# Hash-masked attention and soft MoE on one core: row maxima and logit addends in PSUM, combination weights arranged with the attention, four P buffers

## The chip, the cores and the metric

The kernel runs on one core of a Trainium2 chip. The metric is device time in microseconds from one execution, the median over three runs. The engines are named as the profile names them: PE (matmuls on TensorE) with PEld (its weight loads), DVE (VectorE), ACT (ScalarE), POOL (GpSimd) and SP (SyncE, which issues nearly all transfers). Each engine takes its instructions in the order in which they are written.

## The reference

The inputs are q, k and v of 4 batches x 8 heads x 768 positions x 64 columns, a projection of 64 x 6, and the parameters of a mixture of 8 experts with 4 slots each. All of it is float32.

```python
q_bits = (einsum('bhsd,dk->bhsk', q, proj) > 0)      # k_bits likewise
mask = q_bucket[:, :, :, None] == k_bucket[:, :, None, :]
scores = where(mask, scale * q @ k.T, -1e9)
attn = exp(scores - max) / (sum + 1e-9)
x = (attn @ v)                                       # 3072 x 512, heads side by side
logits = x @ phi                                     # 3072 x 32
d = softmax of logits over the 3072 tokens
slot_input = d.T @ x                                 # 32 x 512
slot_out[e] = relu(slot_input[e] @ w1[e]) @ w2[e]    # 512 -> 1024 -> 512
c = softmax of logits over the 32 slots
out = c @ slot_out                                   # 3072 x 512
```

c are the combination weights of the change: 32 numbers for each of 3072 tokens.

## The kernel before

**Attention.** The 32 heads are worked off one after another, in pairs. A head has six row tiles of 128 positions. `smax` (L370) forms a matrix from queries, keys and hash bits, and DVE reduces each row tile of it to maxima (L373, L376); `shift` (L382 to L385) takes the maximum m of both halves and makes from it the two rows mz that are later subtracted in the matmul itself; `shift_rows` turns mz on PE (L404), casts it on ACT (L407) and moves it into the operand by DMA. `scores` (L419) then forms the scores transposed, with two matmuls each, into one of three PSUM buffers (p_st), and ACT takes the exp from there (L423) into a buffer pt of two row tiles, a P buffer. A head fills three P buffers one after the other. POOL adds the row tiles up (`acc`, L429 and L435), and PE multiplies them with v (`av`, L446). Row sums, their reciprocals and the logits' part of a pair of heads follow in `pair_sum` (L458), `pair_rec` (L465), `pair_turn` (L493), `pair_log` (L473), `pair_add` (L485, L487) and `pair_x` (L508, L510).

**Batches.** After eight heads, `batch_...` functions take that batch into the running softmax over the tokens and the running slot inputs: `batch_max`, `batch_exp` (L620, L622), `batch_turn` (L641, L643), `batch_slots` (L658, L663), and for the combination weights `batch_weigh` (L697, L698) and `batch_share` (L704 to L707). For the last batch the same chain runs behind the last head with nothing beside it: this is called the last head's gap. There 12 and 4 matmuls of `keep_warm` (L249) with unused results stand on PE.

**Soft MoE.** `hidden` (L848), a rectifier, `turned` (L862) and `model` (L930) form the slot outputs; `send` (L951) multiplies them with the combination weights and writes the output. These weights are split into a high and a low part (L878, L879), laid out with 16 bytes of each side by side (`arrange`, L887) and transposed by three matmuls per 384 columns (`turn_weights`, L893, L894), eight times, all between the matmuls of `hidden` and `model`.

**Order.** The order of work is set by hand: every step of a head has a due time in WHEN, in slots of which a head has six (`NT`), and FIRST overrides single ones. The plan is sorted by it and written out. Expert weights are loaded by `load_weights` (L229 and L231, 512 KB each) whenever SBUF becomes free near the end: wb, wy, wp, wl and wc are pools of 5, 6, 3, 5 and 1 such pieces.

**Start.** `first_y` sets constant rows in the operands by a memset (L272) and five DMAs on POOL (L274) from a row of ones; `split_lo` (L294) follows on POOL for the first pair.

Of the kernel before, what the change touches and what calls it, by code (L numbers as in the profile page):

```python
# [34 lines left out]
N_WA, N_WB, N_WY, N_WP, N_WL, N_WC = 23, 5, 6, 3, 5, 1  # L35
# [60 lines left out]
 ('one_sum', 30): 189.395,  # L96
 ('one_log', 30): 188.431,
 ('one_fold', 3): 189.992,
 ('one_turn', 30): 189.777,
 ('one_rec', 30): 190.438,  # L100
 ('one_add', 30): 190.708,
 ('one_x', 30): 191.23,
 ('one_put', 30): 192.78,
 ('acc', 31, 2): 192.109,
 ('av', 31, 2, 0): 191.864,
 ('av', 31, 2, 1): 192.733,
# [6 lines left out]
 ('bits_copy',): -13.916}  # L113
# [34 lines left out]
def lsh_attention_soft_moe(  # L148
# [56 lines left out]
    pts = [held.tile([P, 2 * S], F32, name=f"pt{j}") for j, held in enumerate((ap, lp, mp))]  # L205
# [801 lines left out]
```

## Time and profile before

| | before |
|---|---|
| median of three runs | 516.6 us (516.0 to 517.17) |
| the profiled execution's span | 515.0 us |
| its mean granted TensorE clock | 0.984 |
| PE busy | 494.8 us, 96% |
| POOL busy | 327.6 us, 64% |
| DVE busy | 381.7 us, 74% |
| ACT busy | 241.2 us, 47% |

The profiled execution's own time is its span, from the first instruction to the last; what lies around it is not in the profile. A row of a group gives the busy time and the mean of one in ns, then the engine's idle time ahead of it and what ended it. A row of a timeline gives start and length in microseconds, the instructions run together, and in brackets the idle time ahead.

### The profile page before, as it was taken

The page shows a single profiled execution, that of the slowest core. Times are in us where ns is not written, and L with a number is a line of the kernel's source. Part 1 is how long each engine was busy: PE and PEld are TensorE (multiplying, and loading weights), DVE is VectorE, ACT ScalarE, POOL GpSimd, SP SyncE. Part 2 cuts the span into 40 slices and gives each one's busy share as a digit, 9 for nine tenths or more (in the row PEclk, how much of TensorE's full clock was granted, in tenths as well). Part 3 has the DMA queues.
Part 4 walks back from the last instruction along what each step waited for, and adds up shares of the span by engine and source line. Part 5 has one row for each costly group of instructions (what it writes and reads, how often), then busy time and mean ns, then how long its engine had stood idle before and what let it go on. Part 6 is the DMA issues. An engine that isn't in the chain of part 4 may idle for free.

```text
span 515.0 us, 9100 instructions
## 1 busy us (share of the span) xinstructions
PE 494.8 (96%) x3164; PEld 289.1 (56%) x3164; DVE 381.7 (74%) x703; ACT 241.2 (47%) x463; POOL 327.6 (64%) x223
## 2 busy tenths in 40 slices
PE   6989999999999999999999999999999999999992
PEld 4555556565655555555656555555555655563562
DVE  5585877888888889797887887888877875464233
ACT  4145545454554455554564545454645545422242
POOL 9238776768676867677687867776678686512200
PEclk9789999999999999999999999999999999999997
DMA  5766766758675768586765675867455465869967
GB/s 127 203 137 151 201 161 194 175 163 192 198 161 160 185 186 196 177 191 180 180 191 140 171 197 143 229 146 222 101 145 132 93 169 197 327 264 389 409 270 277
DMA packets 39778, 99.60 MB, mean 193 GB/s; under 512 B 7458, under 2 KB 13732, under 8 KB 39732
## 3 DMA queue, kind: packets, MB, share of 16 engines
q1 hardware_dynamic: 39540, 98.94, 67.8%
q8 instruction: 25, 0.41, 0.3%
q14 instruction: 21, 0.17, 0.1%
q0 software_dynamic: 192, 0.08, 0.1%
HBM read 52.76 MB, written 6.29 MB: 115 GB/s over the span
## 4 chain that ended last, share of the span: by engine, by line
PE 78%; DVE 10%; DMA 5%; SPq 2%; ACT 2%; issue 1%; DVEq 0%; ACTq 0%
PE st L419 23%; PE av L446 21%; PE smx L370 14%; DVE mx L376 3%; PE qs L930 3%; PE qh L848 3%; DMA XY<-w 3%; DVE mx L373 2%; PE mi L458 2%; PE mi L473 2%; PE mi L328 2%; PE mi L508 2%; PE mi L404 1%; SPq L298 1%; DMA w<-w 1%
## 5 line engine op out<-in xcount | busy, mean ns | idle before, releaser
L435 POOL TENSOR_TENSOR acc<-acc,pt 128x768 f32<-128x768 f32 x125 | 238.5, 1908 | 68.5 <-ACT pt L423 54.7
L423 ACT ACTIVATE pt<-st 128x512 f32<-128x512 f32 x288 | 156.6, 596 | 60.5 <-PE st L419 49.3
L419 PE MATMUL st<-XY 128*128 128x256 f32 (+1 forms) x768 | 175.0, 342 | 0.8 <-ACT pt L423 0.5
L376 DVE TENSOR_REDUCE mx<-smx 128x1 f32<-128x512 f32 x192 | 129.4, 682 | 43.6 <-PE smx L370 43.1
L446 PE MATMUL av<-pt,v 128*64 128x384 f32 x768 | 143.1, 501 | 0.0
L419 PEld LDWEIGHTS st<-XY 128*128 128x128 f32 x768 | 123.2, 189 | 19.4 <-ACT pt L423 4.1
L370 PE MATMUL smx<-XY 96*128 96x512 f32 (+1 forms) x384 | 122.9, 374 | 5.2 <-DVE mx L376 3.9
L370 PEld LDWEIGHTS smx<-XY 96*128 96x128 f32 x384 | 65.3, 190 | 55.5 <-issue 16.4
L446 PEld LDWEIGHTS av<-pt,v 128*64 128x64 f32 x768 | 48.2, 137 | 65.7 <-issue 57.6
L429 POOL TENSOR_TENSOR acc<-pt 128x768 f32<-128x768 f32 x32 | 58.3, 1823 | 35.4 <-ACT pt L423 34.9
L373 DVE TENSOR_REDUCE mx<-smx 128x2 f32<-128x512 f32 x96 | 65.2, 679 | 8.5 <-PE smx L370 7.7
L450 ACT COPY avs<-av 128x384 f32<-128x384 f32 x32 | 15.3, 478 | 60.3 <-PE av L446 60.3
L465 DVE RECIPROCAL sm<-sm 128x128 f32<-128x128 f32 x45 | 38.4, 908 | 0.0
L294 DVE TENSOR_TENSOR w<-raw,w 128x768 fp32r<-128x768 f32 x30 | 36.3, 1210 | 1.9 <-ACT w L290 1.7
L407 ACT CAST mr<-mi 12x128 fp32r<-12x128 f32 x31 | 7.9, 254 | 62.7 <-PE mi L404 56.3
L290 ACT CAST w<-raw 128x768 fp32r<-128x768 f32 x32 | 25.1, 831 | 13.7 <-DMA v<-vt 8.2
L510 DVE TENSOR_TENSOR xq<-mi,r 128x256 f32<-128x256 f32 x45 | 17.4, 414 | 2.2 <-PE mi L508 1.2
L487 DVE TENSOR_TENSOR lacc<-lacc,sm 128x384 f32<-128x384 f32 x11 | 18.2, 1656 | 0.4
L321 DVE TENSOR_SCALAR bt<-mi,con 128x384 fp32r<-128x384 f32 x15 | 10.1, 677 | 10.8 <-PE mi L328 7.6
L383 DVE TENSOR_SCALAR mz<-m 128x6 f32<-128x6 f32 x32 | 15.0, 468 | 1.1
L328 PE MATMUL mi<-raw,pb 128*32 128x384 f32 x128 | 15.1, 517 | 0.5 <-DMA raw<-qk 0.5
L930 PE MATMUL qs<-w 128*32 128x256 f32 x232 | 15.2, 382 | 0.0
(173 smaller groups left out, 342.0 us busy)
## 6 DMA issues: line engine op xcount, KB each, us to landing
w<-w SPq DMA_DIRECT2D x61, 512.0 KB
XY<-w SPq DMA_DIRECT2D x63, 384.0 KB
raw<-qk SPq DMA_DIRECT2D x32, 384.0 KB
XY<-w SPq DMA_DIRECT2D x64, 192.0 KB
v<-vt SPq DMA_DIRECT2D x32, 192.0 KB
out<-w SPq DMA_DIRECT2D x12, 512.0 KB
xq<-w SPq DMA_DIRECT2D x3, 512.0 KB
XY<-bt SPq DMA_DIRECT2D x62, 19.5 KB
```

What stands on the lines that cost most here:

```text
L294: (nc.vector if h else nc.gpsimd).tensor_tensor(out=w[:, 2 * x + 1], in0=st[h]["raw"][:, x], in1=w[:, 2 * x], op=ALU.subtract)
L328: nc.tensor.matmul(pts_b[j // 2 if h == 0 else 0][32 * j:32 * j + 32, 0:HC], pb[:, 32 * (j // 2):32 * (j // 2) + 32], st[h]["raw"][:, j // ...
L370: nc.tensor.matmul(pt[:, o:o + b - a], s["Y"][0:96, 0, t * P:(t + 1) * P], s["Y"][0:96, 1, a:b], start=True, stop=True)
L373: nc.vector.tensor_reduce(out=mx[:, n - 1:n + 1], in_=pt.rearrange("p (a x) -> p a x", a=2), axis=AX.X, op=ALU.max)
L376: nc.vector.reduce_max(out=mx[:, n:n + 1], in_=pt, axis=AX.X)
L419: nc.tensor.matmul(pt[:, o:o + b - a], x[:, 1, i * P:(i + 1) * P], x[:, 0, a:b], start=first, stop=not first)
L423: nc.scalar.activation(s["P", i // 2][:, 512 * u:512 * u + 512], pt, AF.Exp, scale=D ** -0.5)
L429: nc.gpsimd.tensor_tensor(out=s["acc"], in0=pr[:, 0:S], in1=pr[:, S:2 * S], op=ALU.add)
L435: eng.tensor_tensor(out=s["acc"], in0=s["acc"], in1=pr[:, a * S:(a + 1) * S], op=ALU.add)
L446: nc.tensor.matmul(s["av"][64 * c:64 * c + 64, 0:HC], s["v"][:, i, :], pr[:, o + c * HC:o + (c + 1) * HC], start=(i == 0), stop=(i == NT - 1))
L465: nc.vector.reciprocal(out=rs[:, k * P:(k + 1) * P], in_=rs[:, k * P:(k + 1) * P])
L930: nc.tensor.matmul(po[32 * j:32 * j + 32], hTs[g][:, f, 32 * j:32 * j + 32], wt[1, x, 2 * g + f // 4, j][:, (f % 4) * HM:(f % 4 + 1) * HM] ...
```

## The change

1. m, the row maximum, is reduced into the last six columns of a PSUM buffer (`p_mi`), which is taken in `shift` and not in `shift_rows`; the turned mz goes to the same buffer. mz is a single tile of 72 columns, of which 12 are written and the rest are zero.
2. The product in `pair_add` is written back to the PSUM buffer it came from, and added from there.
3. Four P buffers take turns over all heads, in place of three per head.
4. `smax` and `scores` are cut into the matmuls and the reductions (`most`) or exps (`exps`), `acc` and `av` into row tiles, each with a due time. A table LAST does for the end what FIRST does for the start.
5. For the first three batches `batch_arrange` lays out the combination weights right after `batch_share`: four casts on ACT and four subtractions on POOL. `batch_spin` transposes them, two groups for each batch, in the last head's gap. The 12 `keep_warm` matmuls there are gone; four stay.
6. Only the last batch's two groups are arranged and transposed in the soft MoE. The pools wp and wl hold one expert weight more each.
7. `first_y` sets its rows by memsets alone. The fold matrix is loaded on SP's queue and not on POOL's.

The diff, cut to its core:

```diff
-N_WA, N_WB, N_WY, N_WP, N_WL, N_WC = 23, 5, 6, 3, 5, 1
+N_P = 4
+N_WA, N_WB, N_WY, N_WP, N_WL, N_WC = 23, 5, 6, 4, 6, 1
...
+ 'batch_arrange': 28.2,
...
+LAST = {('one_sum', -1): 1.725,
...
+ ('batch_spin', -4, 0): 1.7254,
+ ('batch_spin', -4, 1): 3.7251,
+ ('batch_spin', -3, 0): 3.7252,
+ ('batch_spin', -3, 1): 3.7254,
+ ('batch_spin', -2, 0): 3.7256,
+ ('batch_spin', -2, 1): 3.7266,
...
+    mz_wide = mp.tile([P, 72], F32, name="mz")
+    nc.vector.memset(mz_wide, 0.0)
...
-    call = cp.tile([P, B, 3, 2, NS], F32, name="call")
+    call = cp.tile([P, 3, 2, NS], F32, name="call")
+    cts = [cp.tile([P, S], F32R, name=f"ct{b}") for b in range(B - 1)]
...
-        st[h].update((("P", j), pt) for j, pt in enumerate(pts))
-    row = accs[0][0:1]
-    nc.gpsimd.memset(row, 1.0)
+        st[h].update((("P", j), pts[(NT // 2 * h + j) % N_P]) for j in range(NT // 2))
...
     def first_y(i):
-        for ts in (Ys, Xs):
-            nc.gpsimd.memset(ts[i][64:96].bitcast(F32), 0.0)
-        for ts in (Ys, Xs)[i == 0:]:
-            nc.gpsimd.dma_start(out=ts[i][ROW:ROW + 1, 1].bitcast(F32), in_=row)
+        for x in range(2):
+            nc.gpsimd.memset(XYs[i][64:96, x].bitcast(F32), float(x))
...
     def shift(h):
         s = st[h]
-        mz = mp.tile([P, 2 * NT], F32, name="mz", bufs=2)
-        m = mp.tile([P, NT], F32, name="m", bufs=1)
+        mz = mz_wide
+        s["turn"] = p_mi.tile([P, 512], F32, name="mi")
+        m = s["turn"][:, 512 - NT:512]
...
-        pt = p_mi.tile([P, 512], F32, name="mi")
-        nc.tensor.transpose(pt[0:2 * NT, 0:P], s["mz"], ident)
+        pt = s["turn"]
+        nc.tensor.transpose(pt[0:72, 0:P], s["mz"], ident)
...
-            dst = st[h]["rs"]
+            dst = pt[:, 0:HC]
         nc.vector.tensor_tensor(out=dst, in0=pt[:, 0:HC], in1=st[h]["rs"], op=ALU.mult)
...
+    def arrange(ca, n, k0, eng):
+
+        cav = ca.rearrange("p (t j g v i) -> p t j g v i", t=n, j=4, g=2, v=4)
+        src = call.rearrange("p k c s -> p (k c) s")[:, k0:k0 + n].rearrange("p t (g j i) -> p t j g i", g=2, j=4)
+        for g in range(2):
+            for v in (0, 2):
+                nc.scalar.copy(cav[:, :, :, g, v, :], src[:, :, :, g])
+            for v in (1, 3):
+                eng.tensor_tensor(out=cav[:, :, :, g, v, :], in0=src[:, :, :, g], in1=cav[:, :, :, g, 0, :],
+                                  op=ALU.subtract)
+
+    def batch_arrange(b):
+        arrange(cts[b], NT, 0, nc.gpsimd)
+
+    def turn_weights(ca, dst, pool, name):
+        pt = pool.tile([P, 512], F32, name=name)
+        for t in range(3):
+            nc.tensor.matmul(pt[:, t * P:(t + 1) * P], ca[:, t * P:(t + 1) * P], ident_r, start=True, stop=True)
+        nc.scalar.copy(dst, pt[:, 0:HC])
+
+    def batch_spin(b, u, pool):
+        ca = cts[b][:, u * HC:(u + 1) * HC]
+        turn_weights(ca, ca, pool, names[pool])
...
-    at(last + 3.725, keep_warm, 12)
...
+    for b in range(B - 1):
+        for u in range(2):
+            at(last, batch_spin, b, u, p_sm)
+    at(last + 3.727, keep_warm, 4)
...
-            nc.gpsimd.dma_start(out=fold, in_=cst[:, C_FD:C_ALL])
+            nc.sync.dma_start(out=fold, in_=cst[:, C_FD:C_ALL])
...
-    for k in range(1, KC):
-        hidden(hid[1], 1, range(k, k + 1))
-        more_weights(1)
+    hidden(hid[1], 1, range(1, KC))
...
-    more_weights(1)
-    model(pos[0], 0, 1, range(4))
-    more_weights(1)
-    model(pos[0], 0, 1, range(4, FC))
+    model(pos[0], 0, 1)
     so0 = split_out(pos[0], 0)
-    more_weights(1)
-    model(pos[1], 1, 0, range(2))
-    more_weights(1)
-    model(pos[1], 1, 0, range(2, 4))
+    more_weights(0)
+    model(pos[1], 1, 0, range(4))
     more_weights(1)
     send(so0, 0)
```

How the instructions stand. ACT at the end of the third batch, before: the cast of the turned row, the pair's sum (L461), then exps into the P buffers pt.

```order
262 L407 CAST mr<-mi 12x128
263 L461 ACTIVATE sm<-mi,eps 128x384
264 L423 ACTIVATE pt_82<-st 128x512
265 L423 ACTIVATE pt_83<-st 128x512 x2
266 L423 ACTIVATE pt_82<-st 128x512
267 L423 ACTIVATE pt_83<-st 128x512
```

And now (L448, L501 and L466 are the same lines in the changed kernel; ct_118 is the third batch's tile of combination weights):

```order
264 L448 CAST mr<-mi 12x128
265 L501 ACTIVATE sm<-mi,eps 128x384
266 L755 CAST ct_118<-call 128x24x4 x4
267 L466 ACTIVATE pt_84<-st 128x512
268 L466 ACTIVATE pt_81<-st 128x512 x2
269 L466 ACTIVATE pt_84<-st 128x512
270 L466 ACTIVATE pt_81<-st 128x512
```

Four casts stand between the sum and the exps, as at the ends of the first two batches.

PE in the last head's gap, before:

```order
923 L536 MATMUL smx<-ident,sm 128x128 x3
924 L586 MATMUL st<-ident,avs 128x128 x3
925 L551 MATMUL st<-ident,r_4787 32x128 x6
926 L249 MATMUL av<-ident,ones 32x128 x12
927 L641 MATMUL mi<-ident,dl 128x128 x3
928 L249 MATMUL av<-ident,ones 32x128 x4
929 L658 MATMUL st<-xq,sm 32x256 x12
```

And now, with the six transposing groups on L766:

```order
923 L576 MATMUL smx<-ident,sm 128x128 x3
924 L626 MATMUL st<-ident,avs 128x128 x3
925 L766 MATMUL smx<-ident,ct_116 128x128 x3
926 L591 MATMUL st<-ident,r_4752 32x128 x6
927 L766 MATMUL smx<-ident,ct_116 128x128 x3
928 L766 MATMUL smx<-ident,ct_117 128x128 x6
929 L766 MATMUL smx<-ident,ct_118 128x128 x3
930 L681 MATMUL mi<-ident,dl 128x128 x3
931 L766 MATMUL smx<-ident,ct_118 128x128 x3
932 L290 MATMUL av<-ident,ones 32x128 x4
933 L698 MATMUL st<-xq,sm 32x256 x12
```

One group stands ahead of the reciprocals' matmuls, four behind them where keep_warm was, and one behind the transposition of the logits.

ACT in the same gap, before, from the exp (L620) to the copy of the transposed logits (L643):

```order
314 L564 COPY dl<-st 64x384
315 L620 ACTIVATE dl,ml<-dl,run_n_109 64x384
316 L622 ACTIVATE al<-run_n_108,run_n_109 64x1
317 L677 ACTIVATE e<-run_n_109,l 64x1
318 L643 COPY sm<-mi 128x384
```

And now:

```order
317 L604 COPY dl<-st 64x384
318 L767 CAST ct_116<-smx 128x384 x2
319 L767 CAST ct_117<-smx 128x384
320 L660 ACTIVATE dl,ml<-dl,run_n_112 64x384
321 L662 ACTIVATE al<-run_n_111,run_n_112 64x1
322 L767 CAST ct_117<-smx 128x384
323 L767 CAST ct_118<-smx 128x384
324 L717 ACTIVATE e<-run_n_112,l 64x1
325 L683 COPY sm<-mi 128x384
326 L767 CAST ct_118<-smx 128x384
```

Three casts come ahead of the exp, two between the exps and the copy, one behind it.

More of the change, by code (lines that the diff above doesn't have):

```diff
@@ L95 @@
  ('smax', 1, 5, 1): 3.433,
[L96 to L106, printed above, removed]
  ('first_y', 1): -20.551,
@@ L112 @@
  ('bits_rest',): -7.878,
- ('bits_copy',): -13.916}
+ ('bits_copy',): -13.916,
+ ('most', 1, 0): -1.7455,
+ ('most', 1, 2): 0.4525,
+ ('most', 1, 3): 0.5704999999999999,
+ ('most', 1, 4): 1.4785,
+ ('most', 1, 6): 2.0355000000000003,
+ ('most', 1, 7): 2.0615,
+ ('most', 1, 8): 2.2415000000000003,
+ ('most', 1, 10): 2.7745,
+ ('most', 1, 11): 3.4335}
+LAST = {('one_sum', -1): 1.725,
+ ('one_log', -1): 1.7251,
+ ('one_turn', -1): 1.7252,
+ ('one_x', -1): 1.7253,
+ ('one_rec', -1): 1.7255,
+ ('one_add', -1): 1.7256,
+ ('one_put', -1): 3.7252,
+ ('batch_max', -1): 3.7249,
+ ('batch_exp', -1): 3.7253,
+ ('batch_turn', -1): 3.7265,
+ ('batch_scale', -1): 3.7275,
+ ('batch_spin', -4, 0): 1.7254,
[4 more added lines that the diff above has]
+ ('batch_spin', -2, 1): 3.7266,
+ ('one_sum', -2): -2.605,
+ ('one_log', -2): -3.569,
+ ('one_fold', -1): -2.008,
+ ('one_turn', -2): -2.223,
+ ('one_rec', -2): -1.562,
+ ('one_add', -2): -1.292,
+ ('one_x', -2): -0.77,
+ ('one_put', -2): 0.78,
+ ('acc', -1, 1): -2.422,
+ ('acc', -1, 2): -2.051,
+ ('acc', -1, 3): -2.05,
+ ('acc', -1, 4): -0.27500000000000036,
+ ('acc', -1, 5): -0.274,
+ ('av', -1, 0): -2.487,
+ ('av', -1, 1): -2.486,
+ ('av', -1, 2): -0.9130000000000003,
+ ('av', -1, 3): -0.9119999999999999,
+ ('av', -1, 4): -0.13600000000000012,
+ ('av', -1, 5): 0.7329999999999997}
 def constants():
@@ L202, in load @@
         st[h]["raw"] = raw
-    pts = [held.tile([P, 2 * S], F32, name=f"pt{j}") for j, held in enumerate((ap, lp, mp))]
+    at_end = {(NT // 2 * BH - 1 - n) % N_P: held for n, held in enumerate((mp, lp) + (ap,) * (N_P - 2))}
+    pts = [at_end[j].tile([P, 2 * S], F32, name=f"pt{j}") for j in range(N_P)]
+    mz_wide = mp.tile([P, 72], F32, name="mz")
+    nc.vector.memset(mz_wide, 0.0)
     accs = [(mp if i == (BH - 1) % 3 else ap).tile([P, S], F32, name=f"acc{i}") for i in range(3)]
@@ L707, in batch_share @@
         eng.tensor_tensor(out=cb, in0=cb, in1=sm[:, :, :, None].broadcast_to([P, 3, 2, NS]), op=ALU.mult)
+    def arrange(ca, n, k0, eng):
[17 more added lines that the diff above has]
+        turn_weights(ca, ca, pool, names[pool])
     plan = []
+    last = NT * BH
     def at(when, f, *args):
         key = (f.__name__, *(a for a in args if isinstance(a, int)))
-        plan.append((FIRST.get(key, when), len(plan), (f, *args)))
+        if key in FIRST:
+            when = FIRST[key]
+        elif len(key) > 1:
+            back = (key[0], key[1] - (B if f is one_fold or key[0][:5] == "batch" else BH)) + key[2:]
+            when = last + LAST[back] if back in LAST else when
+        plan.append((when, len(plan), (f, *args)))
     first_y(0)
@@ L739, in lsh_attention_soft_moe @@
             at(s0 + WHEN["scores"][x][n], scores, h, n // 2, n % 2)
+            if n % 4 != 1:
+                at(s0 + WHEN["most"][x][n - n // 4 - (n % 4 > 0)], most, h, n)
+                at(s0 + WHEN["exps"][x][n - n // 4 - (n % 4 > 0)], exps, h, n)
         at(s0 + WHEN["shift"][x], shift, h)
         at(s0 + WHEN["shift_rows"][x], shift_rows, h)
-        for j in range(NT // 2):
-            lone = h == BH - 1 and j == NT // 2 - 1
-            at(s0 + (5.725 if lone else WHEN["acc"][x][j]), acc, h, j)
-            if lone:
-                for n in range(2):
-                    at(s0 + 5.85 + n, av, h, j, n)
-            else:
-                at(s0 + (WHEN["av"][x][j] if h < BH - 1 else (3.513, 5.087)[j]), av, h, j)
+        for n in range(NT):
+            if n:
+                at(s0 + WHEN["acc"][x][n - 1], acc, h, n)
+            at(s0 + WHEN["av"][x][n], av, h, n)
         if x and h < BH - 1:
```

148 lines of the change are left out of this document (57 added, 91 removed).

## The prediction

> **What bounds the kernel now.** I read first the busy times and the chain of waits on the page, then a window over the steady attention, then the groups of the lines that the change touches, and last three timelines: a batch's end, the last head's gap, the soft MoE.
>
> ```profile
> PE 494.8 (96%) x3164; PEld 289.1 (56%) x3164; DVE 381.7 (74%) x703; ACT 241.2 (47%) x463; POOL 327.6 (64%) x223
> ...
> PE 78%; DVE 10%; DMA 5%; SPq 2%; ACT 2%; issue 1%; DVEq 0%; ACTq 0%
> ...
> 25.00:400.00 375.00, 371.22 (x2187) 217.48 (x2187) 307.75 (x531) 191.69 (x367) 270.50 (x152) 1.00 0.67 173
> ```
>
> The third row is the window from 25 to 400 us; after the length it gives the busy time of PE, PEld, DVE, ACT and POOL. PE is busy 371.2 of 375.0 us. So in the attention a thing counts only if it takes a matmul away, adds one, or makes PE wait; a faster VectorE or GpSimd alone gives almost nothing. Six microseconds on ACT behind a POOL wait are worth nothing unless PE stands still for them.
>
> The profiled execution has a span of 515.0 us; the three timed runs lie 1.0 to 2.2 us above it (516.0, 516.6, 517.17). I make the sum against 515.0 and add 1.6, the distance of the median.
>
> **Row maxima and addends in PSUM, four P buffers: about 0.**
>
> ```profile
> L487 DVE TENSOR_TENSOR lacc<-lacc,sm 128x384 f32<-128x384 f32 x11 | 18.2, 1656 | 0.4
> L383 DVE TENSOR_SCALAR mz<-m 128x6 f32<-128x6 f32 x32 | 15.0, 468 | 1.1
> L383 DVE TENSOR_SCALAR mz<-m x32: 170/172/973, 18.4 to 431.4; 128x6 f32<-128x6 f32 x32
> 456.19 0.55 DVE L577 TENSOR_TENSOR dl<-dl,st 64x384 f32<-64x384 f32 x1 [1.02 <-PE st L551]
> ACT pt L423 <- POOL acc L435: 5.5, 5, 2.7
> PE st L419 <- ACT pt L423: 0.5, 2, 0.3
> L404 PEld LDWEIGHTS mi<-ident,mz 128*12 128x12 f32 x31 | 2.6, 85 | 21.9 <-DVE mz L385 20.0 <-issue 1.9
> 365.01 0.09 PEld L404 LDWEIGHTS mi<-ident,mz 128*12 128x12 f32 x1 [0.62 <-issue]
> ```
>
> L487 and L383 are the two operations whose operands move to PSUM. Both are slow at times: L383 takes 172 ns at the median and up to 973, L487 1656 on the mean, though the like addition with one operand in PSUM (L577) takes 0.55. If all were fast, VectorE would save 15.0 - 32 x 0.17 = 9.5 us and 18.2 - 11 x 0.55 = 12.1 us. It is busy 307.75 of 375 and is not the bound, so this is an upper end for VectorE's time, not for the span. What PE could get back is the wait of the transposition L404 for mz: 21.9 us in 31, 0.71 each. But at 365.01 it stood for 0.62 with nobody late ("issue"), behind a group of matmuls that write 32 columns each; that much is there in any case. So about 0.1 x 31 = 3 us are VectorE's at most, and part of that is the last row-maximum reduction L376 ahead of them, which stays. I take -0.2, with 0 to -2 as the bounds. The maxima take their PSUM buffer, one of two, when they are reduced and not when they are turned. The bits' matmuls and the pair's sums behind them name no further engine to wait for in the order of the program, so I cost this at nothing; that cover gone, each pair would show a new wait of PE for ACT there.
>
> The fourth P buffer can take away the 5.5 us that exps wait for GpSimd's sums, in five cases. PE's own wait for exps is 0.5 us in two cases, so nothing reached PE: 0, bounds 0 and -0.5.
>
> The wider transposition (72 columns for 12) loads more weights: 85 ns for 12 columns, against
>
> ```profile
> L446 PEld LDWEIGHTS av<-pt,v 128*64 128x64 f32 x760 | 47.8, 137 | 65.4 <-issue 57.3 <-PE smx L370 5.5 <-ACT pt L423 0.9
> L508 PEld LDWEIGHTS mi<-ident,avs 128*128 128x128 f32 x88 | 11.4, 140 | 3.3
> ```
>
> for 64 and 128. So +0.05 each, 31 x 0.05 = 1.6 us if none overlaps the matmul before, 0 if all do; I take +0.5.
>
> **The arrangement after each of three batches: +1.4.** Four casts go on ACT between the pair's sum (L461) and five exps, four subtractions on POOL ahead of the next sums. The end of the third batch before:
>
> ```profile
> 380.95 0.51 POOL L707 TENSOR_TENSOR call<-call,cs 128x192 f32<-128x192 f32 x1 [2.98 <-DVE cs L706]
> ...
> 381.29 0.58 ACT L461 ACTIVATE sm<-mi,eps 128x384 f32<-128x384 f32 x1 [0.52 <-PE mi L458]
> 382.05 2.83 ACT L423 ACTIVATE pt<-st 128x512 f32<-128x512 f32 x5 [0.18 <-PE st L419]
> ...
> 382.92 0.62 PE L419 MATMUL st<-XY 128*128 128x512 f32 x2
> ...
> 383.61 0.64 PE L419 MATMUL st<-XY 128*128 128x512 f32 x2
> ...
> 463.74 0.43 ACT L833 COPY siT<-mi 128x128 f32<-128x128 f32 x2 [3.57 <-PE mi L829]
> ```
>
> Scores have three PSUM buffers. The scores that start at 382.92 need the buffer that the first of the five exps frees; five in 2.83 us are 0.57 each, so that is at 382.62, with 0.30 to spare. ACT is free from 381.87 and idle for 0.18. A cast here is of 96 elements per partition. The nearest row is L833 (128 elements, 0.43 for two, 0.215 each); the strided order may cost more. With c for one cast the first exp starts 4c - 0.18 later and PE waits 4c - 0.48: at 0.22 that is 0.40, at 0.25 0.52. I take 0.45 three times, +1.4. The bounds: c = 0.17 gives 0.2 (+0.6 in all), c = 0.35 gives 0.9 (+2.7). Queued behind the casts are only these exps, and the scores wait for them. The four subtractions delay POOL's sums by about 4 x 0.3 (L707, 192 elements, takes 0.51); cover is the fourth P buffer and POOL's own idle time (270.5 of 375 busy). Without that cover the next exps would wait as they did in the five cases above, and still without PE.
>
> **The last head's gap: +0.7.** Six groups of three transposing matmuls, each with an ACT cast of 384 elements, come in; twelve keep_warm matmuls go.
>
> ```profile
> 458.18 0.61 ACT L620 ACTIVATE dl<-dl,run_n 64x384 f32<-64x384 f32 x1 [3.59 <-DVE run_n L616]
> ...
> 459.10 0.29 ACT L677 ACTIVATE e<-run_n,l 64x1 f32<-64x1 f32 x1
> 459.70 0.48 ACT L643 COPY sm<-mi 128x384 f32<-128x384 f32 x1 [0.31 <-PE mi L641]
> ...
> 455.90 2.78 PE L249 MATMUL av<-ident,ones 128*32 128x128 f32 x24
> 459.06 0.55 PE L641 MATMUL mi<-ident,dl 128*128 128x128 f32 x3 [0.37 <-ACT dl L620]
> ...
> 460.24 0.42 PE L658 MATMUL st<-xq,sm 128*32 128x256 f32 x3
> ```
>
> The chain runs exp (L620), transposition (L641), copy (L643), slots (L658). Three casts fit into ACT's 3.59 us of idle time. Two stand between the exps and the copy: from 459.1 they take 2 x 0.48 (the same size as L643), then e 0.29 and the copy at 460.4 instead of 459.70: +0.7. Bounds: 0.3, if e and the copy close up, and 1.5, if the transposing matmuls also push L641 by one group of 0.55.
>
> **The start: -0.4.** The diff drops a row of ones and five small transfers that POOL issued.
>
> ```profile
> 8.87 3.69 POOL L294 TENSOR_TENSOR w<-raw,w 128x768 fp32r<-128x768 f32 x2
> 25.68 1.57 ACT L290 CAST w<-raw 128x768 fp32r<-128x768 f32 x2 [0.40 <-DMA XY<-w]
> ```
>
> POOL's L294 would be about 1.5 us earlier, but of the work behind it only the cast at 25.68 waits on a transfer, for 0.40. So -0.4, between 0 and -1.1.
>
> **The soft MoE: -3.7.** Six of its eight groups of transposing matmuls (L893) leave.
>
> ```profile
> 475.66 1.92 PE L848 MATMUL qh<-w,siT 128*32 128x512 f32 x16
> 477.52 0.55 PE L893 MATMUL qa<-ident,avs 128*128 128x128 f32 x3
> 478.00 1.92 PE L848 MATMUL qh<-w,siT 128*32 128x512 f32 x16
> ...
> 490.25 1.07 PE L930 MATMUL qs<-w 128*32 128x256 f32 x16
> 491.25 0.55 PE L893 MATMUL qa<-ident,avs 128*128 128x128 f32 x3
> 491.73 1.07 PE L930 MATMUL qs<-w 128*32 128x256 f32 x16
> ```
>
> From 475.66 to 478.00 is 2.34 for sixteen matmuls and one group. In the run of 80 that begins here
>
> ```profile
> 463.58 8.79 PE L848 MATMUL qh<-w,siT 128*32 128x512 f32 x80
> ```
>
> sixteen take 1.72 (8 x 0.215: 8.6 us in 80 is 0.1075 each). So one group costs 2.34 - 1.72 = 0.62; from 490.25 to 491.73 it is 1.48 - 0.86 = 0.62 again. Six: -3.7. Behind them the output transfers shift as they stand. Two more weights are loaded early, so two fewer must land late; if landing set the end all the same, I would keep perhaps half, -1.9, and that is the upper bound. The rows follow one another without a DMA wait on PE, which speaks against it.
>
> The sum: -3.7 + 1.4 + 0.7 + 0.5 - 0.4 - 0.2, and +0.3 (0 to 0.5) for the fold matrix, which now loads on SP's queue behind twelve weights: **-1.4**. 515.0 - 1.4 = 513.6 for the span, **515.2 us** for the median. As the bounds will not all be met on one side, I give the forecast itself 1.4 either way, 513.8 to 516.6.
>
> **The clock in the gap.** Does PE keep its full clock without the twelve keep_warm matmuls?
>
> ```profile
> 6.90:10.30 3.40, 2.60 (x23) 2.11 (x18) 2.74 (x5) 2.01 (x4) 3.27 (x4) 1.00 0.29 60
> 10.30:13.70 3.40, 1.65 (x4) 0.71 (x5) 3.37 (x6) 0.00 (x0) 3.34 (x4) 0.99 0.63 123
> 13.70:20.50 6.80, 5.92 (x20) 3.27 (x21) 3.65 (x8) 0.00 (x0) 2.79 (x4) 0.50 0.70 191
> 27.40:30.80 3.40, 1.86 (x7) 1.15 (x7) 3.40 (x7) 0.82 (x2) 1.80 (x1) 0.99 0.63 121
> 30.80:34.20 3.40, 3.40 (x11) 0.98 (x12) 2.34 (x6) 0.00 (x0) 0.00 (x0) 0.51 0.48 101
> 455.90:459.30 3.40, 3.03 (x30) 2.76 (x27) 2.62 (x8) 1.11 (x4) 0.00 (x0) 1.00 1.03 416
> ```
>
> Behind PE's busy time and those of the others stands the granted clock. Stretches with 1.65 and 1.86 of 3.40 us busy are followed by half clock, the one with 2.60 is not. In the gap it is 3.03 now; four groups of 0.5 to 0.55 in place of 2.78 us of keep_warm make about 2.4, between the two and nearer 2.60. A drop would halve the clock for 3.4 us of nearly full work, up to 1.7 us.
>
> The Trainium skill's page "TensorE: Matmul & The Clock Gate" (Part 1, The HAM clock gate) has a free-running window of about 3.4 us, after one idle one of which the clock is halved, and the section Why this matters for your kernels asks for no idle gaps over about 3 us between bursts. The 3.4 us agree with the rows; but here the clock fell with PE busy half the time, so the idle-gap rule alone is too lenient. By that rule the term is 0, by the rows 0 with a risk of 1.7.
>
> **Rivals.** Against the median of 516.6:
> A, the casts hide and the gap absorbs its own: the batch stall is 0.2 x 3, the gap 0.3, the wider weights and the fold nothing, and PSUM gives back 0.7: -3.7 + 0.6 + 0.3 - 0.4 - 0.7 = -3.9, 512.7 us. For it: the 0.30 to spare and ACT's 0.18 of idle time; against it: ACT takes its queue in order.
> B, the gap grows: three groups on PE (3 x 0.55) and two casts (0.96) all fall on the chain, +2.6 in place of 0.7. Then -1.4 + 1.9 = +0.5, 517.1. For it: the groups share two PSUM buffers, each freed by a cast on ACT; against it: ACT's 3.59 us of idle time.
> C, the slower side: ACT's arrangement costs more. At c = 0.5, what the 384 elements of L643 take, PE waits 4 x 0.5 - 0.48 = 1.5 at each of three batches, +4.6 in place of 1.4. Then -1.4 + 3.2 = +1.8, 518.4. It decides from c = 0.44 on, where the sum passes +1.0. For it: pieces of sixteen bytes at a stride, which no row shows on ACT; against it: L833's 0.215 for more elements.
> D, the clock falls in the gap: -1.4 + 1.7 = +0.3, 516.9.
>
> **How the numbers follow.** Forecast 0.45, A 0.24, B 0.12, C 0.11, D 0.08. A difference of 0.2%, 1.0 us, is about what a measurement of this kernel can tell from none. Faster: 0.29 of the forecast's 0.45 (its value is 0.4 beyond the line) and all of A, 0.53. Within: 0.13 of the forecast, 0.10 of B, 0.05 of D, 0.28. Slower: 0.03 of the forecast, 0.02 of B, 0.03 of D, all of C, 0.19. The time is the forecast's, 515.2. The range takes in A's 512.7 and nearly reaches C, 512.3 to 518.2; left out are C's far end and a gain by PSUM on top of A.
>
> **What would show it.** Right: the time between the first hidden matmul (L848) and the last output matmul (L951) falls by 3.7; at each of three batches' ends the five exps start about 0.7 later and PE waits 0.3 to 0.9 for one; the copy ahead of L658 comes 0.7 later after the exp L620. If L383 and L487 fall to 0.17 and 0.55 while the pairs of heads take as long as before, PSUM freed VectorE and not the kernel; if the pairs get shorter by 0.1 or more, this step is wrong. Wrong as a whole: a granted clock under 1.0 behind 455 us (D), casts over 0.4 each (C), no wait of PE at the batches (A), or the soft MoE no shorter.

## The result and the profile after

| | before | changed |
|---|---|---|
| median of nine runs each | 516.57 us (514.75 to 517.42) | 513.37 us (512.31 to 515.12) |
| ratio | 1 | 0.9941, 95% interval 0.9925 to 0.9956 |
| the profiled execution's span | 515.04 us | 510.30 us |
| from the first hidden matmul to the last output matmul | 41.85 us | 38.14 us |
| from the last head's row sums to the first hidden matmul | 11.13 us | 11.69 us |
| from the last output matmul to the end | 9.61 us | 8.80 us |

The change makes the kernel 3.1 us faster (2.3 to 3.9), where 1.4 was forecast. The two profiled executions are 4.7 us apart, so part of that belongs to these two executions. The recorded spans lie 2.0 us under the times in the changed kernel, and 1.7 to 1.8 in the other runs of the kernel before. By that the profiled execution of before (515.0) lay 0.2 above its median; the one of the changed kernel, at 512.31, is the fastest of its nine and 1.1 under the median.

From the page of the changed kernel, the busy times and the chain, and then the window from 25 to 400 us (length, then busy time of PE, PEld, DVE, ACT, POOL):

```profile
PE 491.0 (96%) x3140; PEld 287.7 (56%) x3140; DVE 358.0 (70%) x674; ACT 242.3 (47%) x481; POOL 322.3 (63%) x200
...
PE 83%; DVE 9%; DMA 3%; ACT 2%; issue 1%; SPq 0%; DVEq 0%; ACTq 0%
...
25.00:400.00 375.00, 371.67 (x2190) 218.42 (x2190) 290.66 (x532) 193.35 (x379) 274.30 (x164) 1.00 0.65 172
```

PE is still the bound. VectorE has lost 17 us in the window (307.75 to 290.66) and the window holds three matmul records more than before. The attention got hardly shorter: from the second transposition of mz to the last it takes 384.95 us, against 385.24.

The soft MoE, PE's timeline: the last row of before, then the changed kernel.

```profile
505.43 0.39 PE L951 MATMUL qa<-w 128*128 128x256 f32 x2
```

```profile
463.36 8.79 PE L911 MATMUL qh<-w,siT 128*32 128x512 f32 x80
472.08 1.09 PE L925 MATMUL qa<-ident,w 128*128 128x128 f32 x8
473.10 5.36 PE L911 MATMUL qh<-w,siT 128*32 128x512 f32 x48
...
486.45 0.55 PE L766 MATMUL qa<-ident,avs 128*128 128x128 f32 x3
...
501.50 0.40 PE L983 MATMUL qa<-w 128*128 128x256 f32 x2
```

The 48 matmuls that were cut by three groups before now run through. 501.50 - 463.36 is 38.14, against 505.43 - 463.58 = 41.85: 3.71 less, six times 0.62.

Where an execution stands is easiest read off the transposition of mz, once per head (L404, now L445). It begins with the first one 0.88 us earlier than before, with the second 0.49, and with the last one, at 431, 0.79. In between the pairs without a batch's end gain about 0.1 each, and each of the three batches' ends loses 0.4. Two of these rows before, and the same two now:

```profile
217.25 0.08 PEld L404 LDWEIGHTS mi<-ident,mz 128*12 128x12 f32 x1 [0.75 <-DVE mz L385]
231.68 0.09 PEld L404 LDWEIGHTS mi<-ident,mz 128*12 128x12 f32 x1 [0.63 <-DVE mz L385]
```

```profile
216.62 0.11 PEld L445 LDWEIGHTS mi<-ident,mz 128*72 128x72 f32 x1 [0.74 <-DVE mz L426]
230.93 0.11 PEld L445 LDWEIGHTS mi<-ident,mz 128*72 128x72 f32 x1 [0.62 <-issue]
```

The interval from the odd head's to the next even head's went from 14.43 to 14.31. PE's wait ahead of the transposition is as long as before (0.62 for 0.63), with "issue" where mz stood, so the gain lies elsewhere. VectorE in that interval, before and now (timelines):

```profile
226.18 1.72 DVE L487 TENSOR_TENSOR lacc<-lacc,sm 128x384 f32<-128x384 f32 x1
227.83 0.68 DVE L376 TENSOR_REDUCE mx<-smx 128x1 f32<-128x512 f32 x1
...
230.02 0.95 DVE L383 TENSOR_SCALAR mz<-m 128x6 f32<-128x6 f32 x1
```

```profile
225.58 0.56 DVE L527 TENSOR_TENSOR lacc<-lacc,mi 128x384 f32<-128x384 f32 x1
226.59 0.69 DVE L416 TENSOR_REDUCE mx<-smx 128x1 f32<-128x512 f32 x1 [0.45 <-PE smx L406]
...
229.42 0.16 DVE L424 TENSOR_SCALAR mz<-mi 128x6 f32<-128x6 f32 x1
```

The addition takes 0.56 for 1.72 and the maximum's comparison 0.16 for 0.95. Before, the reduction (L376) followed the slow addition without a gap; now it waits 0.45 for PE. So VectorE had been late there, and PE, which needs one of two smx buffers back, waited for it. In the kernel before, the weight load of the L370 matmul that takes the buffer begins right behind the end of that reduction (228.51), after a wait of 0.09 that the trace puts down to L376:

```profile
228.56 0.19 PEld L370 LDWEIGHTS smx<-XY 96*128 96x128 f32 x1
```

### The profile page after: what moved, and what is told of

Read it like the earlier page. It is cut to its first block, busy times and chain, and to the rows that moved or that the text cites. A ratio compares the mean times of both kernels' runs of the same rounds, so it can differ in the third digit from the quotient of the medians.

```text
span 510.3 us, 8930 instructions
## 1 busy us (share of the span) xinstructions
PE 491.0 (96%) x3140; PEld 287.7 (56%) x3140; DVE 358.0 (70%) x674; ACT 242.3 (47%) x481; POOL 322.3 (63%) x200
## 4 chain that ended last, share of the span: by engine, by line
PE 83%; DVE 9%; DMA 3%; ACT 2%; issue 1%; SPq 0%; DVEq 0%; ACTq 0%
PE st L460 24%; PE av L486 22%; PE smx L406 14%; DVE mx L416 3%; PE qs L962 3%; PE qh L911 3%; PE mi L365 2%; DVE mx L413 2%; PE mi L498 2%; PE mi L513 2%; PE mi L548 2%; PE mi L445 2%; DMA w<-w 1%; PE av L290 1%; PE mi L698 1%; DMA XY<-w 1%
## 5 line engine op out<-in xcount | busy, mean ns | idle before, releaser
L466 ACT ACTIVATE pt<-st 128x512 f32<-128x512 f32 x288 | 156.5, 596 | 58.3 <-PE st L460 54.5
L406 PE MATMUL smx<-XY 96*128 96x512 f32 (+1 forms) x384 | 121.6, 371 | 5.1 <-DVE mx L416 3.8
L331 DVE TENSOR_TENSOR w<-raw,w 128x768 fp32r<-128x768 f32 x30 | 37.8, 1259 | 1.0 <-ACT w L327 1.0
L448 ACT CAST mr<-mi 12x128 fp32r<-12x128 f32 x31 | 7.9, 254 | 64.0 <-PE mi L445 53.3
L327 ACT CAST w<-raw 128x768 fp32r<-128x768 f32 x32 | 25.1, 831 | 12.6 <-DMA XY<-w 6.9
L445 PEld LDWEIGHTS mi<-ident,mz 128*72 128x72 f32 x31 | 3.5, 114 | 21.6 <-DVE mz L426 12.8
L548 PE MATMUL mi<-ident,avs 128*128 128x128 f32 x90 | 14.8, 272 | 0.0
```

The lines of the kernel that those rows point to most:

```text
L331: (nc.vector if h else nc.gpsimd).tensor_tensor(out=w[:, 2 * x + 1], in0=st[h]["raw"][:, x], in1=w[:, 2 * x], op=ALU.subtract)
L406: nc.tensor.matmul(pt[:, o:o + b - a], s["Y"][0:96, 0, t * P:(t + 1) * P], s["Y"][0:96, 1, a:b], start=True, stop=True)
L466: nc.scalar.activation(s["P", n // 4][:, 512 * u:512 * u + 512], s["st_ps", n - (n % 4 == 2)], AF.Exp, scale=D ** -0.5)
```

## The experiments

Two accounts stood against each other for the attention. P: the PSUM operands shorten VectorE's queue where PE waits for a maximum. W: the wider transposition or the fourth P buffer shortens the pairs. For the end there were also two, D (the clock falls in the last head's gap) and its contrary.

### The addends alone, on the kernel before

```diff
-            dst = st[h]["rs"]
+            dst = pt[:, 0:HC]
```

> The kernel before with one edit: pair_add writes its product back to the PSUM buffer and adds from there. Theory P (PSUM addends are the part of the gain that the prediction made too small): VectorE's L487 falls from 1.66 us to 0.55 in eleven pairs, the row maxima queued behind it come earlier, and the interval from an odd head's L404 to the next even head's falls by 0.15 in each of these pairs, so about -1.7 us in all. Rival W (the wider transposition and the fourth P buffer shortened the pairs): L487 falls as well, but the interval stays at 14.43 and the time is that of before.

Measured: 515.5 against 516.18 us, ratio 0.9988 (0.9974 to 1.0002), too near to 1 for the timing alone to show it. The weight loads of two transpositions, and between them the one of L370 that began at 228.56 before:

```profile
217.08 0.09 PEld L404 LDWEIGHTS mi<-ident,mz 128*12 128x12 f32 x1 [0.74 <-DVE mz L385]
228.25 0.19 PEld L370 LDWEIGHTS smx<-XY 96*128 96x128 f32 x1
231.37 0.09 PEld L404 LDWEIGHTS mi<-ident,mz 128*12 128x12 f32 x1 [0.63 <-DVE mz L385]
```

14.29 where it was 14.43, in nine pairs: -1.3 us, with 12 columns and three P buffers. From the first transposition to the load of L370 it is 11.17 and not 11.31, so the gain is all there by then. Account P holds for the addends. L487 takes 553 or 554 ns in each of eleven.

### The addends back in SBUF

```diff
-            dst = pt[:, 0:HC]
+            dst = st[h]["rs"]
```

> The changed kernel with the product of pair_add back in SBUF. Theory P: the odd-to-even interval goes from 14.31 back to 14.47, so +1.9 us in all (12 pairs), and L487's line back to 1.66 us. Rival W: no change of the interval, 0 +- 0.3 us by the profile.

Measured: 514.61 us, 0.9966 (0.9948 to 0.9983). The addition is back at 1645 ns on the median, and the interval is 14.38 for 14.31: +0.07 a pair, half of what the edit is worth on the kernel before. P in kind, not in size; why the two differ was not tried.

### The maxima back in SBUF

```diff
-        m = s["turn"][:, 512 - NT:512]
+        m = mp.tile([P, NT], F32, name="m", bufs=1)
```

> The changed kernel with only the row maximum m back in SBUF (the turned row's buffer is taken as in the change). If m's place counts, the transposition of the odd heads waits up to 0.3 longer where it did before (0.78 and 0.93 at two of them), +0.5 us in all; if it does not, 0 +- 0.2, since L383 was slow (up to 973 ns) only where PE had other work.

Measured: 515.02 us, 0.9981 (0.9967 to 0.9995). The line that compares the maximum, and the transposition behind the second batch's end:

```profile
L424 DVE TENSOR_SCALAR mz<-m x32: 170/171/1582, 17.7 to 430.8; 128x6 f32<-128x6 f32 x32
```

```profile
285.81 0.11 PEld L445 LDWEIGHTS mi<-ident,mz 128*72 128x72 f32 x1 [0.90 <-DVE mz L426]
```

Its longest is now 1582 ns; in the changed kernel it is 165. PE waits 0.90 for mz behind a batch and not 0.62. The intervals there are 14.87 to 14.90 against 14.67, and the one that ends at 419 is 14.01 against 13.53 (13.98 in the kernel before): 3 x 0.21 + 0.48 = 1.1 us, at four places, twice what was expected and not where it was expected. Other intervals are as in the changed kernel or 0.03 shorter. By the timing the edit costs more, about 2.1 us (0.9981 against 0.9941, with intervals apart); where the rest lies is not shown.

### Twelve columns of mz

```diff
-        nc.tensor.transpose(pt[0:72, 0:P], s["mz"], ident)
+        nc.tensor.transpose(pt[0:2 * NT, 0:P], s["mz"][:, 0:2 * NT], ident)
```

> The changed kernel with 12 columns of mz turned and not 72. By the weight loads (113 ns against 85) and the even-to-odd interval, which is 11.74 with 72 and 11.70 with 12, the narrow one gains 0.03 to 0.04 per odd head, -0.6 us in all. Rival: the width is what shortens the odd-to-even interval by 0.12; then it is +0.12 x 14 = +1.7 us with 12 columns.

Measured: 513.34 us, 0.9949 (0.9925 to 0.9974).

```profile
204.96 0.09 PEld L445 LDWEIGHTS mi<-ident,mz 128*12 128x12 f32 x1 [0.62 <-issue]
216.67 0.09 PEld L445 LDWEIGHTS mi<-ident,mz 128*12 128x12 f32 x1 [0.74 <-DVE mz L426]
230.92 0.09 PEld L445 LDWEIGHTS mi<-ident,mz 128*12 128x12 f32 x1 [0.62 <-issue]
```

11.71 and 14.25, against 11.75 and 14.31: the width costs 0.04 in one half and 0.03 to 0.06 in the other, about 1.2 us in fifteen pairs. The rival falls, and of W the width is out. The finer due times of the change were not tried alone; but a pair here, 14.25 + 11.71, is within 0.04 of the one with the addends alone on the kernel before, 14.29 + 11.71. The median does not show this 1.2; the profile has the clock drop told of below, and nine runs from 510.03 to 515.91 hide it easily.

### Three P buffers

```diff
-N_P = 4
+N_P = 3
```

> The changed kernel with three P buffers in turn instead of four. If the fourth buffer counts nothing for PE, as predicted, ACT's waits for POOL's sums come back (5.5 us before in five cases; more here, since the arrangement delays POOL's sums by 1.2 us at three batches), and the intervals of the pairs stay, 0 +- 0.3 us. If it is what covers the arrangement, PE waits at the three batches' ends up to 1.2 longer each, +1 to +3.5 us.

Measured: 514.59 us, 0.9971 (0.9952 to 0.9991). ACT's waits for POOL's sums are 1.3 us in four cases, against 0.8 in two with four buffers (1.5 in three in a second profile of the changed kernel, told of below):

```profile
ACT pt L466 <- POOL acc L477: 1.3, 4, 0.4
```

The interval at the third batch's end is 14.65 against 14.66, and the last transposition comes at 431.25 against 431.05. In the attention the fourth buffer is worth nothing that the trace shows, and W is out. The median is 1.2 us higher, with intervals that overlap; the execution profiled had the clock drop told of below. Whether the third buffer costs anything elsewhere stays open.

### The arrangement behind the exps

```diff
- 'batch_arrange': 28.2,
+ 'batch_arrange': 30.0,
```

> The changed kernel with batch_arrange due behind the five exps and not ahead of them. If the four casts cost what was predicted by standing ahead of the exps (0.52 per batch as measured: 14.67 against 14.31 and against 14.27 for the same interval of the kernel before, which has 0.12 less of gain), the interval behind each of three batches falls from 14.67 to 14.15, so -1.5 us in all. If it is POOL's subtractions or the casts' load as such, the interval stays at 14.5 to 14.7.

Measured: 512.08 us, 0.9926 (0.9897 to 0.9955). ACT at the end of the third batch, in the changed kernel and here:

```profile
380.59 0.58 ACT L501 ACTIVATE sm<-mi,eps 128x384 f32<-128x384 f32 x1 [0.57 <-PE mi L498]
381.08 0.78 ACT L755 CAST ct<-call 128x96 fp32r<-128x96 f32 x4
381.75 2.72 ACT L466 ACTIVATE pt<-st 128x512 f32<-128x512 f32 x5
```

```profile
380.11 0.58 ACT L501 ACTIVATE sm<-mi,eps 128x384 f32<-128x384 f32 x1 [0.57 <-PE mi L498]
380.81 2.82 ACT L466 ACTIVATE pt<-st 128x512 f32<-128x512 f32 x5
383.52 0.78 ACT L755 CAST ct<-call 128x96 fp32r<-128x96 f32 x4
```

```profile
378.90 0.11 PEld L445 LDWEIGHTS mi<-ident,mz 128*72 128x72 f32 x1 [0.74 <-DVE mz L426]
393.19 0.11 PEld L445 LDWEIGHTS mi<-ident,mz 128*72 128x72 f32 x1 [0.62 <-issue]
```

The interval (the last two rows, of this kernel) is 14.29 to 14.33 at the three batches, against 14.66: the place of the arrangement costs 0.35 each time, 1.0 us in all. 0.52 had been expected; 0.12 of that compared with a gain of the addends that the first pair of a batch does not have, since it has no addition. The edit moves POOL's subtractions too, but the wait is for ACT. Here is the weight load of the scores that need the buffer of the first exp, in the changed kernel and in this one:

```profile
382.40 0.30 PEld L460 LDWEIGHTS st<-XY 128*128 128x128 f32 x2 [0.53 <-ACT pt L466]
```

```profile
381.46 0.41 PEld L460 LDWEIGHTS st<-XY 128*128 128x128 f32 x2
```

From the start of the pair's sum to the first exp it is 1.16 us in the changed kernel and 0.70 here, where the exp waits for no cast.

### The transposing groups back in the soft MoE

```diff
-    for b in range(B - 1):
-        for u in range(2):
-            at(last, batch_spin, b, u, p_sm)
...
-    hidden(hid[1], 1, range(1, KC))
+    for k in range(1, KC):
+        hidden(hid[1], 1, range(k, k + 1))
+        batch_spin((k - 1) // 2, (k - 1) % 2, q_a)
...
```

The other three follow between the parts of `model`.

> The changed kernel with the six transposing groups of the first three batches back between the matmuls of the soft MoE, in the order of before, and nothing in their place in the last head's gap (four keep_warm matmuls stay, the twelve stay away). MoE: 6 x 0.62 = +3.7 us between its first matmul and its last. Gap: -0.56, what the groups cost there, if the clock stays at full speed. PE then idles 3.0 us on end in the gap; if a window with less than 1.65 of 3.4 us busy halves the clock, as at 10 to 14 us, the clock reads 0.5 behind the gap and the slots' and fold's matmuls take up to 1.7 us longer.

Measured: 517.79 us, 1.0023 (1.0001 to 1.0045). The soft MoE takes 41.60, +3.46. The gap is 13.97, and its rows read like this (PE's timeline, then two windows; behind the busy times stands the granted clock, the share of TensorE's full clock):

```profile
458.98 0.90 PE L681 MATMUL mi<-ident,dl 128*128 128x128 f32 x3 [2.99 <-ACT dl L660]
459.81 1.70 PE L290 MATMUL av<-ident,ones 128*32 128x128 f32 x7
```

```profile
456.80:460.20 3.40, 1.22 (x5) 0.86 (x6) 2.84 (x11) 1.41 (x5) 0.00 (x0) 0.68 1.02 416
460.20:463.60 3.40, 3.40 (x27) 2.03 (x27) 1.13 (x7) 0.26 (x1) 0.00 (x0) 0.50 0.51 197
```

The clock was at half for 6.8 us from 458.1 on, and L681 takes 0.90 and not 0.55. The gap is 2.84 longer than in the kernel before, which has the same matmuls and twelve more: PE idled 2.99 us on end, the clock fell, and the two together are the price.

### Without the last four keep_warm matmuls

```diff
-    at(last + 3.727, keep_warm, 4)
```

> The changed kernel without the last four keep_warm matmuls. In the gap ACT's copy ahead of L698 ended at 459.71 and PE began L698 at 459.99, behind the keep_warm matmuls. If the gap's cost is PE's queue (the sixth group and keep_warm), L698 comes 0.2 to 0.3 earlier; if it is the two casts ahead of the copy, as predicted, L698 does not move. Total -0.2 +- 0.2 us, not to be told by the timing.

Measured: 513.62 us, 0.9945 (0.9924 to 0.9966).

```profile
460.29 1.92 PE L698 MATMUL st<-xq,sm 128*32 128x256 f32 x24 [0.38 <-ACT sm L683]
```

L698 starts 8.09 after the row sums, against 8.32: the 0.23 were PE's own queue (the sixth group and keep_warm). What remains of the delay against before (7.79) is 0.30, the wait for ACT's copy. The prediction had all 0.7 on ACT. The whole gap is 11.33, against 11.69.

### The changed kernel again

> The changed kernel once more, for a second profile and as the measure for the two others. Its first profile kept the full clock through the last head's gap (11.69 from the row sums to the first hidden matmul, 11.13 before); of six kernels with the same gap but for a detail, five show half clock for 3.4 us near 457 to 461 and a gap of 12.9 to 13.4. Theory D (the rival D of the prediction is true in most executions, by where the clock's window falls): this profile shows the drop too, or the timed runs spread over 1.5 us or more, their median near 513.4. Theory N (the drop belongs to the edits): full clock again.

Measured: 513.41 us, 0.9945 (0.9927 to 0.9962), the first median again. The profile is another one. First L681 in the first profile, then the rows of this one:

```profile
458.28 0.55 PE L681 MATMUL mi<-ident,dl 128*128 128x128 f32 x3 [1.01 <-ACT dl L660]
```

```profile
457.95 0.90 PE L681 MATMUL mi<-ident,dl 128*128 128x128 f32 x3 [1.01 <-ACT dl L660]
458.51 0.90 PE L766 MATMUL smx<-ident,ct 128*128 128x128 f32 x3
459.34 1.70 PE L290 MATMUL av<-ident,ones 128*32 128x128 f32 x7
460.62 0.65 PE L698 MATMUL st<-xq,sm 128*32 128x256 f32 x3
```

```profile
454.70:458.10 3.40, 2.16 (x19) 1.68 (x14) 2.62 (x8) 1.87 (x6) 0.00 (x0) 0.98 1.03 410
458.10:461.50 3.40, 3.40 (x23) 2.78 (x25) 1.89 (x11) 1.81 (x5) 0.00 (x0) 0.52 0.74 294
```

Half clock for 3.4 us, L681 at 0.90, and 13.01 from the row sums to the first hidden matmul, against 11.69 in the first profile of the very same kernel. So the drop needs no edit, and theory N falls. Seven profiles have this gap unchanged. In six of them the clock fell there (the addends and the maxima back in SBUF, 12 columns, three P buffers, the late arrangement, and this one), with gaps of 12.89 to 13.37; in the first profile of the changed kernel it did not. It did not fall without the last four keep_warm matmuls either. PE was busy 2.15 to 2.46 of the 3.4 us ahead of a fall, but stretches with 2.0 and 2.4 went by without one; so PE's busy time alone does not tell which way it goes.

How often the drop comes in the timed executions is another matter. The record has the mean granted clock of each, and 3.4 us more at half clock lower it by 0.003. Of the fourteen timed executions of the changed kernel, seven lie at 0.978 to 0.982 (two of the first nine, and all five here) and seven at 0.984 or 0.985. In the timed executions behind those seven profiles, 31 of 57 lie at 0.982 or below; in the kernel before, 22 of 80. A longer stretch at half clock at the start, which this profile has too, lowers the mean as much. So the drop may come in about half of the executions, and that it comes in most is not shown. Nor are those with the lower clock longer: the median of their spans is 511.3 us, that of the other seven 511.5.

The two profiles of the changed kernel show how much else moves. The second one is 0.84 later at the second transposition, 1.18 shorter from there to the last (in one pair, 13.81 for 15.33, ACT's cast L327 does not wait for a transfer as it did in the first profile, for 2.31), and 1.32 longer in the gap: 1.0 in all.

### The gap filled

```diff
- ('batch_spin', -3, 1): 3.7254,
+ ('batch_spin', -3, 1): 3.72525,
  ('batch_spin', -2, 0): 3.7256,
- ('batch_spin', -2, 1): 3.7266,
+ ('batch_spin', -2, 1): 3.72562,
+ ('batch_drop', -2, 0): 3.7268,
+ ('batch_drop', -2, 1): 3.7269,
...
-    at(last + 3.727, keep_warm, 4)
+    at(last + 3.72561, keep_warm, 3)
+    at(last + 3.7266, keep_warm, 2)
```

`batch_spin` of the third batch issues its matmuls alone, and `batch_drop` the cast that follows.

> The changed kernel with another order in the last head's gap: the fourth group's cast ahead of the exp, the sixth group ahead of the logits' transposition, the casts of the third batch behind the copy; three keep_warm matmuls between the fifth and sixth group and two ahead of the slots, none behind. PE is then busy about 3 of any 3.4 us there, as in the kernel before. Theory D: no half clock in the profile, the gap 11.1 to 11.4, and the median 1.0 to 1.5 us under that of the changed kernel (0.3 to 0.5 by the order, 1.5 in about two thirds of the executions by the clock). Theory N: only the 0.3 to 0.5 by the order.

Measured: 513.15 us, 0.9941 (0.9922 to 0.9960), 0.3 under the changed kernel on the same chip, where theory D asked for 1.0 to 1.5. L681 to L698 ran at full clock, and the slots began 7.83 after the row sums, as early as before. The profiled execution, at 516.57, is the slowest of the nine (the others took 512.31 to 513.83), and it shows a new wait, in VectorE's and PE's timeline:

```profile
463.92 0.29 DVE L731 TENSOR_SCALAR fold<-fold,li 128x128 f32<-128x128 f32 x1 [1.98 <-DMA fold<-cst]
```

```profile
461.71 1.25 PE L700 MATMUL st<-xq,sm 128*32 128x256 f32 x12
464.74 1.13 PE L907 MATMUL mi<-fold,run_x 128*128 128x128 f32 x8 [1.79 <-DVE run_x L705]
```

The fold matrix landed late behind its twelve weights, PE stood for 1.79, and the clock fell at 466.1, in the soft MoE (39.85 for 38.14). In this execution the gain at one place was given back at the next. The expectation had not asked what came due behind the slots. But VectorE's 1.98 is the longest wait for the fold matrix of all profiles (0.43 to 1.76 in the others that load it there), and seven of the other eight executions have a mean clock of 0.984 to 0.986. So they seem to have kept the full clock and still gained little; the price that theory D put on the drop does not show in the median, and why is open.

### All three

> The gap as in the run before it, batch_arrange behind the five exps, and 12 columns of mz: -1.0 for the arrangement (three times 0.34), -0.6 for the width, so 1.6 under the kernel with the filled gap and 2.6 to 3.1 us under the changed kernel. If the late arrangement or the width only moved a wait, less than 0.8 of it stays.

Measured: 509.75 us, 0.9868 (0.9845 to 0.9891), 3.7 us under the changed kernel on the same chip and 3.4 under the filled gap alone, where 1.6 had been expected. 0.2 of it lies outside the spans, which are 1.8 us under the times here and 2.0 in those two kernels; the rest of the surplus is not explained. The gap is 11.25, the batches' intervals 14.26 to 14.29, the other pairs 11.68 + 14.26, the last transposition comes at 429.24, and the clock is whole from 22.5 to 503.8 us, behind the last matmul. VectorE still waited 0.56 for the fold matrix, PE 0.36.

### The fold matrix early

```diff
-            fold = tp.tile([P, P], F32, name="fold")
-            nc.sync.dma_start(out=fold, in_=cst[:, C_FD:C_ALL])
+        if slot == last - 15:
+            nc.sync.dma_start(out=fold, in_=cst[:, C_FD:C_ALL])
...
+    fold = cp.tile([P, P], F32, name="fold")
...
-    mz_wide = mp.tile([P, 72], F32, name="mz")
+    mz_wide = mp.tile([P, 2 * NT], F32, name="mz")
```

> The kernel of the run with all three edits, and the fold matrix loaded some ten heads' slots earlier into a place of its own, ahead of the last expert weights on SP's queue and not behind twelve of them (mz is 12 columns wide in memory too, which makes room). If the late fold matrix holds up the gap (VectorE waited 0.56 for it in the run with all three, 1.98 in the one with the filled gap alone, where the fold matmuls came 1.79 late and the clock fell behind it), the gap is 10.9 to 11.2 and VectorE does not wait; the median falls by 0.3 to 0.8. If the wait was covered by run_x, which needs the slots, the median stays within 0.3.

Measured: 509.81 us, 0.9876 (0.9849 to 0.9902).

```profile
458.42 0.28 DVE L732 TENSOR_SCALAR fold<-fold,li 128x128 f32<-128x128 f32 x1
```

VectorE no longer waits, the gap is 11.01 for 11.25, and the profiled execution is the shortest of those profiled, 507.6. In the medians, taken on two chips, the 0.24 do not show. Both kernels beat the changed one and the one before, by 6.4 to 6.8 us against the latter.

## Why the prediction was right, and where it was not

The direction was right and the time lay in the range; the likeliest sum was 1.7 us short. 513.37 is below the 513.8 to 516.6 that the forecast itself was given, and nearer to rival A's 512.7; but what A put together (casts that hide, nothing for the wider transposition) is not what the runs show. That the range held owes something to luck: errors of two signs met. Step by step, the sum of 515.0 against 510.3:

| term | predicted | shown |
|---|---|---|
| six groups out of the soft MoE | -3.7 | -3.71 in the profile, +3.46 when put back |
| arrangement at three batches | +1.4 | +1.0 |
| PSUM operands | -0.2 (0 to -2) | -0.6 to -1.3 for the addends, -1.1 for the maxima, by the intervals |
| wider transposition | +0.5 (0 to 1.6) | about +1.2 |
| last head's gap | +0.7 | +0.56 at full clock, +1.9 with the drop |
| start | -0.4 | -0.49 in this pair of profiles, not settled |
| fold matrix | +0.3 | 0 in the two profiles of the changed kernel |
| tail | 0 | -0.81 |

**The soft MoE** came out to the hundredth, since the rows of before hold the group's price twice, with and without it, on the engine that is the bound.

**The arrangement.** The formula for the wait, 4c - 0.48, needs the distance between two casts. The exp behind the four starts 0.67 after the first cast (381.75 and 381.08), so c is 0.17, though one cast takes 0.26 from start to end. The first exp came 0.46 later and not 0.7, and the formula gives 0.20 for PE, the lower bound; 0.35 was measured. The mechanism was right: PE waits for that exp. Of the 0.35, 0.24 stand ahead of the first matmul of these scores; 0.11 come behind it, where the second matmul starts 0.34 and not 0.23 after the first, which the formula had nothing for. Rival C asked for a c of 0.44 and falls.

**PSUM** is the step that failed: "-0.2, with 0 to -2 as the bounds". It was -1.7 to -2.4, at the far end and beyond, and by the sign that the prediction itself had named (pairs shorter by 0.1 or more) the step is wrong: with the addends alone a pair is 0.14 shorter. The argument looked at PE's wait at L404 alone and split it into 0.62 that is there anyway and a rest. The waits for the smx buffers, which the slow addition holds up through the reductions behind it, lie at L370 in front, as waits of a tenth; 0.14 in nine pairs does not stand out in any group's idle time. And the maxima count in the pair that ends at 419 and at the batches' ends. There the comparison takes up to 1.58 with m in SBUF and the arrangement ahead, and 0.97 in the kernel before, whose intervals there are 14.27 or 14.28; that the arrangement moves POOL's work onto it is the likely reason. The price of one part of the change depended on another, which a sum of terms cannot hold.

**The wider transposition** was taken at a third of its upper bound and cost three quarters of it.

**The gap.** The mechanism was only partly right: the delay of 0.53 ahead of the slots was 0.23 of PE's own queue and 0.30 of ACT's casts. Rival D, given 0.08, "the clock falls in the gap", is what six of seven profiles show, and the prediction had named it as a sign of being wrong as a whole. Its price was 1.7, and the profiles show 1.2 to 1.7. Its time, 516.9, did not come about: PSUM and the tail had gained as much on the other side, and in the timed executions the drop does not show as a longer time. So forecast and rival D both held in part. By the idle-gap rule of the page "TensorE: Matmul & The Clock Gate" of the Trainium skill (Why this matters for your kernels) the clock would have stayed full here, since PE never idled for more than 1.01 on end in this gap. The rows of 10 to 31 us had spoken against that rule, and they were right.

**The tail.** Nothing in the prediction spoke of it: from the last output matmul to the end it is 9.61 and 9.62 in the two profiles with the old end, and 8.79 to 8.81 in all twelve with the new one. In the two old traces an 8 KB packet of an instruction queue falls into the last output transfers, and a few of their packets end 0.6 us behind the others; in the twelve there is none. That this packet is the cause was not tried.

**The start.** The second transposition comes at 46.60 and 47.23 in the two profiles with the old start and between 45.97 and 47.40 in twelve with the new one; the spread is as large as the term.

The shown terms add up to -3.95 to -4.65 for the first pair of profiles, with the gap at full clock, against -4.7. The medians differ by 3.2, since the profiled execution of the changed kernel was the fastest of its nine. What sets it apart is open: six of the other eight have a mean clock as high as its own, within 0.001, and take up to 2.8 us more.

## What to carry to other kernels

A wait of a tenth of a microsecond at an in-order bound engine does not appear in any list of waits, but it repeats: compare the interval between two marks of the same kind, pair by pair, before a slow operation of another engine is costed at nothing. When filler matmuls are taken out, price the clock at every place where PE waits behind them, and look at more than one profile: the same program showed full clock and half clock in the same gap. Hold what a profile shows against the timed executions: the drop costs 1.2 to 1.7 us in the profiles, and filling the gap brought 0.3 in the median. When a wait is taken out of a chain, ask what lands next; in the profile of the filled gap the late fold matrix held PE for 1.79.

## What was not expected of the hardware

A VectorE operation on six columns took up to 0.97 us, and 1.58 with the arrangement in, when both its operands lay in SBUF and POOL was at work, and 170 to 172 with POOL idle; with one in PSUM, 162 to 165 ns in all 32. An addition of 384 columns went from 1003 to 1732 ns to 553 to 555 by the same step.

The granted clock fell to half for 3.4 us with PE busy 2.15 to 2.46 of the 3.4 us ahead, with no idle stretch over 1.01 us, in six of seven profiles of nearly the same gap. Four casts that follow one another on ACT took 0.78 us, though one alone has 0.26, and the exp behind them started 0.67 after the first.
